# Three of eight experts' output matmuls in two float32r parts, with the two halves of PSUM added on GpSimd

## The chip, the cores and the metric

The kernel runs on one NeuronCore of one Trainium2 chip. The metric is the device time of one execution in microseconds (us), smaller is better. Five engines work beside one another, each through its own queue in order: TensorE (PE in the profile, with its weight loads as PEld), VectorE (DVE), ScalarE (ACT), GpSimd (POOL) and SyncE (SP), which here only issues DMA transfers.

## The reference, cut to what matters

```python
# x: (4, 4160, 192), weight_gen: (4, 4160, 8, 7)
w = softmax(weight_gen, axis=-1)                       # 7 taps, 8 heads
x_pad = concatenate([zeros(B, 6, D), x], axis=1)
out = einsum('bshk,bskhg->bshg', w, x_unf)             # 7 shifted rows of x, 24 channels a head
x = out.reshape(B, S, 192)

h = maximum(x @ w_in, 0.0)                             # 192 -> 1024
conv_out = sum_k conv_w[k] * hp[:, k:k + S, :]         # 3 taps along the sequence
gate = 1.0 / (1.0 + exp(-conv_out))
return (h * gate) @ w_out                              # 1024 -> 192
```

Everything is float32. What the change's name calls experts are the eight slices (NF = 8) of 128 columns into which the kernel cuts the 1024 hidden columns; `f` counts them.

## The kernel before

The 16640 positions lie on 128 partitions with 130 positions each (SEG). One step `j` handles four positions of every partition (R = 4), 512 columns once they are transposed; there are 33 steps (NB).

**Attention, step q.** `load_x` brings rows of x into `ring`, a ring of 24 rows (RING), and `load_w` brings the tap weights of two steps into one of four buffers (WB = 4), where `sm_ops` makes the softmax. `tap` (L292) multiplies rows of the ring by a tap's weights: seven products a step, in steps q >= 3 all on GpSimd. Two accumulating DMAs (`fold1`, `fold2`, issued by GpSimd) and one GpSimd addition (`fold3`, L325) sum the seven products, PE transposes the sum (L340, 6 matmuls a step), and `split_hi` (ACT, L360) and `split_lo` (DVE, L364) leave it as a pair of float32r tiles, H the rounded values and L what the rounding left.

**Unit (j, f).** `mm1` (L378) makes 128 hidden columns for 512 positions with five float32r matmuls of 512 columns into one of five PSUM buffers `z` (NZ = 5). Then `relu` (ACT, L384) writes h, `wmid` (ACT, L388) the middle tap of the convolution back into z, `conv_side` twice (DVE, L395) the side taps, `sig` (ACT, L402) a tanh, and `gmul` (DVE, L411) the gated value into `g` in SBUF, which frees z. `carry` (SP, L416) copies the last two rows of h to where the next step needs them.

**Output tile (j, i).** For each of a step's four positions `mm2` (L424) adds up eight float32 matmuls, one for each slice f, with 128 columns of g as the stationary operand and 192 columns of `wo` as the moving one. A float32 matmul is two MATMUL records in the trace, so a tile has 16. `evac` (ACT, L433) copies the tile from PSUM to `o` with a factor 0.5, and `store` (SP, L437) writes the four tiles of a step. Two PSUM buffers (`ops`, `dps`) take turns.

**Order.** All of this is first collected as tasks with a duration and dependences (`task`, durations from `vec`, `act`, `pool` and constants such as `d_ = 0.03 + NF * 0.326` for an output tile), a list scheduler places the tasks, and the instructions are issued in that order, which is fixed from then on. Tiles of step j are ranked at j + 1.62 (`WO_`), attention of step q at q - 2.7 (`TO`). A task of kind "VK" holds both DVE and GpSimd in the plan.

Of the kernel before, what the change touches and what calls it, by code (L numbers as in the profile page):

```python
# [35 lines left out]
WB = 4  # L36
ROUNDS = 1
RING = 24
CG = 2
CH = (  # L40
# [11 lines left out]
def vec(n, ps=1):  # L52

    return 0.07 + n / 960 + 0.06 * ps
# [11 lines left out]
def kernel(  # L66
# [37 lines left out]
    o_p = ctx.enter_context(tc.tile_pool(name="o", bufs=4))  # L104
# [10 lines left out]
    wh, wl = wi[:, 0], wi[:, 1]  # L115
    wo = const.tile([P, NF, D], F32, name="wo")
    h = const.tile([P, NF, R + 2, P], F32, name="h")
# [248 lines left out]
    z_t, g_t = {}, {}  # L366
# [36 lines left out]

    def g_of(j, f):
        if j not in g_t:
            g_t[j] = g_p.tile([P, NF, W], F32, tag="g", name="g")
        return g_t[j][:, f, :geom(j)[0] * P]
# [12 lines left out]
    def mm2(j, i, ps=None):  # L420
        if ps is None:
            ps = (ps_d if i % 2 else ps_o).tile([P, W], F32, tag="dps" if i % 2 else "ops", name="ops")
        for f in range(NF):
            nc.tensor.matmul(  # L424
                out=ps[:, 0:D], lhsT=g_of(j, f)[:, i * P:(i + 1) * P], rhs=wo[:, f, :],
                start=(f == 0), stop=(f == NF - 1),
            )
        return j, i, ps

    def evac(j, i, ps):  # L430
        if i == 0:
            o_t[j] = o_p.tile([P, R, D], F32, tag="o", name="o")
        nc.scalar.activation(out=o_t[j][:, i, :], in_=ps[:, 0:D], func=ACTF.Copy, scale=0.5)  # L433

    def store(j, a, b):
        c0 = R * j - 2 if j else 0
        nc.sync.dma_start(  # L437
            out=os_[:, (c0 + a) * D:(c0 + b) * D], in_=o_t[j][:, a:b].rearrange("p s d -> p (s d)")
        )
# [3 lines left out]
    with tc.manual_schedule():  # L443
        stage = g_p.tile([P, NF, W], I32, tag="g", name="stage").rearrange("p f w -> p (f w)")
        r_in = stage[:, 0:2 * FF].rearrange("p (c b) -> p c b", b=2)
        r_fold = stage[:, 2 * FF:3 * FF].rearrange("p (c b) -> p c b", b=2)
        r_cw = stage[0:3 * NF, 3 * FF:3 * FF + 2 * P].rearrange("p (c b) -> p c b", b=2)
        r_out = [o_p.tile([P, 2 * D, 2], I32, tag="o", name="r_out") for _ in range(4)]
# [206 lines left out]


# [69 lines left out]
        zl, last_mm, mm_end = [], [None], {}  # L726

        def unit(j, f):
# [13 lines left out]
            rd[n] = gm[n] = task("V", vec(m_, 0), [t_] + dep, lambda: gmul(j, f))  # L742
            zl.append(gm[n])
# [9 lines left out]
        def out_tiles(j):  # L753
            d_ = 0.03 + NF * 0.326
            no = geom(j)[0]
            for i in range(no):
# [4 lines left out]
                def fn(i=i, hold=hold, z_=z_):  # L761
# [3 lines left out]
                    "P", d_, [rd[j * NF + f] for f in range(NF)] + wo_rdy + dep, fn,  # L765
# [162 lines left out]
```

## Time and profile before

| what | value |
|---|---|
| median of 3 runs | 706.98 us (706.78 to 707.1) |
| span of the profiled execution | 704.3 us, 10972 instructions |
| what lies around the span, by the median | 2.7 us (706.98 - 704.3) |
| PE busy | 683.6 us, 97% |
| DVE busy | 629.0 us, 89% |
| ACT busy | 554.5 us, 79% |
| POOL busy | 514.9 us, 73% |

The profiled execution has no time of its own beside its span; the median of the runs less the span is taken for what lies around it. The span is what the trace covers, from the first to the last instruction. Busy times are unions of the recorded durations; the records of neighbouring instructions on an engine can overlap, so the distance from one start to the next is often shorter than the recorded duration.

### The profile page before, as it was taken

What the parts mean: (1) busy time and instruction counts of PE and PEld (TensorE: products, weight loads), DVE (VectorE), ACT (ScalarE), POOL (GpSimd) and SP (SyncE); (2) the same over time, 40 slices, a digit from 0 to 9 for tenths busy, and PEclk for the clock granted to TensorE, in tenths of its full rate; (3) what the DMA queues carried; (4) which work ended last, traced back from release to release, by engine and by line L of the source; (5) the groups of instructions that cost most, each with busy time, mean ns of one, the idle gap of its engine ahead of it and who ended that gap; (6) DMA issues with size and microseconds to landing.
All of it is one profiled execution on the core that took longest, in us unless ns stands there. A gap on an engine that the chain in (4) does not pass through costs nothing.

```text
span 704.3 us, 10972 instructions
## 1 busy us (share of the span) xinstructions
PE 683.6 (97%) x3749; PEld 623.3 (89%) x3749; DVE 629.0 (89%) x1005; ACT 554.5 (79%) x1079; POOL 514.9 (73%) x422
## 2 busy tenths in 40 slices
PE   1899999999999999999999999999999999999998
PEld 1788999999999999999999999999999999999998
DVE  6999999999999999999899899988898888888881
ACT  3588888887888888878787787888878778888881
POOL 3998987998999888897776878877777788730000
PEclk9999999999999999999999999999999999999999
DMA  7736998999999888797988889788888887781211
GB/s 236 214 92 166 218 205 207 211 226 213 207 223 217 202 199 194 178 207 170 218 190 201 197 163 223 176 213 193 189 188 184 177 184 167 171 194 67 78 44 45
DMA packets 70787, 127.59 MB, mean 181 GB/s; under 512 B 5046, under 2 KB 42573, under 8 KB 70732
## 3 DMA queue, kind: packets, MB, share of 16 engines
q0 software_dynamic: 20160, 58.99, 47.5%
q1 hardware_dynamic: 50090, 67.51, 29.6%
q8 instruction: 29, 0.48, 0.3%
q10 hardware_dynamic: 482, 0.40, 0.2%
q14 instruction: 26, 0.21, 0.1%
HBM read 20.51 MB, written 12.78 MB: 47 GB/s over the span
## 4 chain that ended last, share of the span: by engine, by line
PE 96%; DVE 2%; DMA 1%; POOL 0%; issue 0%; ACT 0%; POOLq 0%
PE ops L424 47%; PE z L378 43%; PE tp L340 4%; PE ops L340 1%; DMA stage<-in_moe_conv_w_dram 1%; PE z L424 1%; DMA stage<-in_moe_w_in_dram 0%; DVE py L292 0%; POOL px L292 0%; POOL py L292 0%; DVE r L257 0%; DVE m L248 0%; DVE w L242 0%; DVE px L292 0%; DVE dps L146 0%
## 5 line engine op out<-in xcount | busy, mean ns | idle before, releaser
L395 DVE SCALAR_TENSOR_TENSOR z<-h,cw,z 128x512 f32<-128x512 f32 (+1 forms) x528 | 377.6, 742 | 21.6 <-ACT z L388 15.7
L424 PE MATMUL ops<-wo,g 128*128 128x192 f32 x2048 | 353.1, 326 | 0.0
L424 PEld LDWEIGHTS ops<-wo,g 128*128 128x128 f32 x2048 | 338.9, 190 | 9.8
L378 PE MATMUL z<-H,wi 128*128 128x512 f32 x1056 | 303.8, 409 | 1.0 <-ACT wi L614 1.0
L292 POOL TENSOR_TENSOR px<-ring,w 128x768 f32<-128x768 f32 (+2 forms) x146 | 230.9, 1698 | 67.2 <-PE tp L340 67.0
L378 PEld LDWEIGHTS z<-H,wi 128*128 128x128 f32 x1056 | 191.1, 188 | 32.8 <-ACT wi L614 1.4
L402 ACT ACTIVATE z<-z 128x512 f32<-128x512 f32 (+1 forms) x264 | 150.7, 571 | 53.4 <-DVE z L395 51.7
L411 DVE SCALAR_TENSOR_TENSOR g<-z,h 128x512 f32<-128x512 f32 (+1 forms) x264 | 177.0, 678 | 12.3 <-ACT z L402 10.3
L388 ACT ACTIVATE z<-h,cw 128x512 f32<-128x512 f32 (+1 forms) x264 | 179.7, 684 | 6.2
L384 ACT ACTIVATE h<-z 128x512 f32<-128x512 f32 x264 | 155.4, 591 | 15.8 <-PE z L378 15.6
L292 POOL TENSOR_TENSOR py<-ring,w 128x768 f32<-128x768 f32 (+2 forms) x108 | 163.3, 1826 | 2.2 <-DMA px<-py 2.2
L378 PE MATMUL z<-L,wi 128*128 128x512 f32 x264 | 103.0, 390 | 0.0
L325 POOL TENSOR_TENSOR px<-px 128x512 f32<-128x512 f32 (+1 forms) x60 | 72.9, 1466 | 5.3 <-DMA px<-px 5.3
L360 ACT ACTIVATE H<-tp 64x256 fp32r<-64x256 f32 (+1 forms) x93 | 42.3, 454 | 22.0 <-PE tp L340 21.7
L378 PEld LDWEIGHTS z<-L,wi 128*128 128x128 f32 x264 | 49.5, 188 | 11.2
L433 ACT ACTIVATE o<-ops 128x192 f32<-128x192 f32 x128 | 42.1, 329 | 19.2 <-PE ops L424 16.7
L318 POOL DMA_DIRECT2D px<-px x30 | 36.7, 1224 | 15.3 <-DMA px<-py 12.9
L315 POOL DMA_DIRECT2D px<-py x30 | 40.4, 1346 | 8.5 <-POOL py L292 8.5
L340 PE MATMUL tp<-ident,px 128*128 128x128 f32 x228 | 38.0, 281 | 2.8 <-POOL px L292 2.0
L340 PEld LDWEIGHTS tp<-ident,px 128*128 128x128 f32 x228 | 30.0, 145 | 8.7 <-POOL px L292 2.5
L364 DVE TENSOR_TENSOR H<-tp,H 64x256 fp32r<-64x256 f32 x60 | 25.4, 423 | 7.7 <-ACT H L360 5.8
L364 DVE TENSOR_TENSOR L<-tp,H 128x512 fp32r<-128x512 f32 x33 | 22.7, 688 | 8.7 <-ACT H L360 8.6
(67 smaller groups left out, 181.4 us busy)
## 6 DMA issues: line engine op xcount, KB each, us to landing
px<-py POOLq DMA_DIRECT2D x30, 1152.0 KB, 9.9
h<-h SPq DMA_DIRECT2D x128, 256.0 KB, 4.4
px<-px POOLq DMA_DIRECT2D x30, 768.0 KB, 6.6
ring<-in_x_dram SPq DMA_DIRECT2D x31, 384.0 KB, 6.7
out_dram<-o SPq DMA_DIRECT2D x31, 384.0 KB, 5.8
w<-in_weight_gen_dram SPq DMA_DIRECT2D x15, 224.0 KB, 6.0
r_out<-in_moe_w_out_dram SPq DMA_DIRECT2D x4, 384.0 KB, 5.6
wi<-scr SPq DMA_DIRECT2D x8, 128.0 KB, 6.2
```

The lines of the kernel that those rows point to most:

```text
L292: eng.tensor_tensor(out=dst[:, a:b, :].rearrange("p s (h g) -> p s h g", g=GRP), in0=ring[:, p:p + n, :].rearrange("p s (h g) -> p s h g", ...
L325: nc.gpsimd.tensor_tensor(out=dst.rearrange("p (s d) -> p s d", s=R), in0=a[:, :, lo:hi], in1=b[:, :, lo:hi], op=ALU.add)
L340: nc.tensor.matmul(o, lhsT=a, rhs=ident, is_transpose=True, start=(start and c == 0), stop=(stop and c == len(ops) - 1))
L360: nc.scalar.activation(out=hi, in_=src, func=ACTF.Copy)
L364: nc.vector.tensor_tensor(out=lo, in0=src, in1=hi.bitcast(F32), op=ALU.subtract)
L378: nc.tensor.matmul(out=z, lhsT=w[:, fs], rhs=h_t[j, nm], start=(i == 0), stop=(i == len(terms) - 1))
L384: nc.scalar.activation(out=hrow(f, 2, R), in_=z_t[j, f], func=ACTF.Relu)
L388: nc.scalar.activation(out=z_t[j, f][:, :no * P], in_=hrow(f, cc, no), func=ACTF.Copy, scale=cw[:, NF + f:NF + f + 1])
L395: nc.vector.scalar_tensor_tensor(out=z, in0=hrow(f, cc + d, no), scalar=cw[:, k * NF + f:k * NF + f + 1], in1=z, op0=ALU.mult, op1=ALU.add,)
L402: nc.scalar.activation(out=z, in_=z, func=ACTF.Tanh, scale=0.5)
L411: nc.vector.scalar_tensor_tensor(out=g_of(j, f), in0=z_t[j, f][:, :no * P], scalar=1.0, in1=hrow(f, cc, no), op0=ALU.add, op1=ALU.mult)
L424: nc.tensor.matmul(out=ps[:, 0:D], lhsT=g_of(j, f)[:, i * P:(i + 1) * P], rhs=wo[:, f, :], start=(f == 0), stop=(f == NF - 1),)
```

## The change

In steps 2 to 31 (`FIRST = 2`, `LAST = 1`) the matmuls of `mm2` for f = 0, 1, 2 (`NS = 3`) are no longer float32. `w_split` cuts the weights of these slices once into `wos`: a rounded float32r part (ACT) and the rest (DVE). `g_hi` (ACT) rounds the gated value to float32r, `g_lo` subtracts to get the rest, on DVE for f = 0 and 1 and on GpSimd for f = 2 (`GL = "VVG"`). Each slice then takes two float32r matmuls: the rounded part of g against both parts of the weights side by side (384 columns), and the rest of g against the rounded weights (192 columns, added to the first half). The tile's result so stands in two halves of 192 columns; `evac` copies both, and `join` adds them on GpSimd before `store`. For f = 0 and 1 `gmul` writes back into z in PSUM, which stays taken until `g_lo`; for f = 2 it writes into a scratch tile. To find room in SBUF the ring has 20 rows in place of 24, the tap weights three buffers in place of four, and `o` two buffers of double size in place of four.

```diff
--- before.py
+++ after.py
@@ -33,10 +33,14 @@
 NX = 3
 NY = 2
 NZ = 5
-WB = 4
+WB = 3
 ROUNDS = 1
-RING = 24
+RING = 20
 CG = 2
+NS = 3
+GL = "VVG"
+FIRST = 2
+LAST = 1
 CH = (
     ("f", 0, 256, 5.2, "VGP", "G"),
     ("m", 0, 256, 8.7, "VVP", "G"),
@@ -101,7 +105,8 @@
     py_p = ctx.enter_context(tc.tile_pool(name="py", bufs=NY))
     t_p = ctx.enter_context(tc.tile_pool(name="t", bufs=2))
     g_p = ctx.enter_context(tc.tile_pool(name="g", bufs=2))
-    o_p = ctx.enter_context(tc.tile_pool(name="o", bufs=4))
+    gx_p = ctx.enter_context(tc.tile_pool(name="gx", bufs=2))
+    o_p = ctx.enter_context(tc.tile_pool(name="o", bufs=2))
     ps_z = ctx.enter_context(tc.tile_pool(name="ps_z", bufs=NZ, space=bass.MemoryType.PSUM))
     ps_t = ctx.enter_context(tc.tile_pool(name="ps_t", bufs=1, space=bass.MemoryType.PSUM))
     ps_o = ctx.enter_context(tc.tile_pool(name="ps_o", bufs=1, space=bass.MemoryType.PSUM))
@@ -113,7 +118,9 @@
     cw = const.tile([P, 3 * NF], F32, name="cw")
     wi = const.tile([P, 2, 2, FF], F32R, name="wi")
     wh, wl = wi[:, 0], wi[:, 1]
+    NP = NF - NS
     wo = const.tile([P, NF, D], F32, name="wo")
+    wos = const.tile([P, NS, 2, D], F32R, name="wos")
     h = const.tile([P, NF, R + 2, P], F32, name="h")
     cw_raw = h[0:3 * NF, 0, R, :]
     ring = const.tile([P, RING, D], F32, name="ring")
@@ -363,7 +370,7 @@
         for src, hi, lo in parts(q, part, tp, pairs):
             nc.vector.tensor_tensor(out=lo, in0=src, in1=hi.bitcast(F32), op=ALU.subtract)
 
-    z_t, g_t = {}, {}
+    z_t, g_t, gs_t, gx_t = {}, {}, {}, {}
 
     def geom(j):
         no = R if j else R - 2
@@ -401,10 +408,42 @@
         z = z_t[j, f][:, :geom(j)[0] * P]
         nc.scalar.activation(out=z, in_=z, func=ACTF.Tanh, scale=0.5)
 
+    def halves(j):
+        return FIRST <= j < NB - LAST
+
+    def split(j, f):
+        return f < NS and halves(j)
+
+    def gx_of(j, f, b):
+        if j not in gx_t:
+            gx_t[j] = gx_p.tile([P, NS, 2, W], F32R if halves(j) else F32, tag="gx", name="gx")
+        return gx_t[j][:, f, b, :geom(j)[0] * P]
+
     def g_of(j, f):
+        if split(j, f):
+            if GL[f] == "G":
+                n = gs_t.setdefault((j, f), len(gs_t))
+                return scr[n % 2][:, n // 2 % 3].bitcast(F32)
+            return z_t[j, f]
+        if f < NS:
+            return gx_of(j, f, 0)
         if j not in g_t:
-            g_t[j] = g_p.tile([P, NF, W], F32, tag="g", name="g")
-        return g_t[j][:, f, :geom(j)[0] * P]
+            g_t[j] = g_p.tile([P, NP, W], F32, tag="g", name="g")
+        return g_t[j][:, f - NS, :geom(j)[0] * P]
+
+    def g_hi(j, f):
+        nc.scalar.activation(out=gx_of(j, f, 0), in_=g_of(j, f), func=ACTF.Copy)
+
+    def g_lo(j, f):
+        (nc.vector if GL[f] == "V" else nc.gpsimd).tensor_tensor(
+            out=gx_of(j, f, 1), in0=g_of(j, f), in1=gx_of(j, f, 0).bitcast(F32), op=ALU.subtract
+        )
+
+    def wo_hi():
+        nc.scalar.activation(out=wos[:, :, 0], in_=wo[:, 0:NS], func=ACTF.Copy)
+
+    def wo_lo():
+        nc.vector.tensor_tensor(out=wos[:, :, 1], in0=wo[:, 0:NS], in1=wos[:, :, 0].bitcast(F32), op=ALU.subtract)
 
     def gmul(j, f):
         no, cc = geom(j)
@@ -420,32 +459,44 @@
     def mm2(j, i, ps=None):
         if ps is None:
             ps = (ps_d if i % 2 else ps_o).tile([P, W], F32, tag="dps" if i % 2 else "ops", name="ops")
+        c = slice(i * P, (i + 1) * P)
+        terms = []
         for f in range(NF):
-            nc.tensor.matmul(
-                out=ps[:, 0:D], lhsT=g_of(j, f)[:, i * P:(i + 1) * P], rhs=wo[:, f, :],
-                start=(f == 0), stop=(f == NF - 1),
-            )
+            if split(j, f):
+                terms.append((2 * D, gx_of(j, f, 0)[:, c], wos[:, f].rearrange("p b d -> p (b d)")))
+                terms.append((D, gx_of(j, f, 1)[:, c], wos[:, f, 0]))
+            else:
+                terms.append((D, g_of(j, f)[:, c], wo[:, f, :]))
+        for n, (m, g, w) in enumerate(terms):
+            nc.tensor.matmul(out=ps[:, 0:m], lhsT=g, rhs=w, start=(n == 0), stop=(n == len(terms) - 1))
         return j, i, ps
 
     def evac(j, i, ps):
         if i == 0:
-            o_t[j] = o_p.tile([P, R, D], F32, tag="o", name="o")
-        nc.scalar.activation(out=o_t[j][:, i, :], in_=ps[:, 0:D], func=ACTF.Copy, scale=0.5)
+            o_t[j] = o_p.tile([P, 2, R, D], F32, tag="o", name="o")
+        n = 2 if halves(j) else 1
+        nc.scalar.activation(
+            out=o_t[j][:, 0:n, i, :], in_=ps[:, 0:n * D].rearrange("p (b d) -> p b d", b=n), func=ACTF.Copy, scale=0.5
+        )
+
+    def join(eng, j, a, b):
+        o = o_t[j]
+        eng.tensor_tensor(out=o[:, 0, a:b], in0=o[:, 0, a:b], in1=o[:, 1, a:b], op=ALU.add)
 
     def store(j, a, b):
         c0 = R * j - 2 if j else 0
         nc.sync.dma_start(
-            out=os_[:, (c0 + a) * D:(c0 + b) * D], in_=o_t[j][:, a:b].rearrange("p s d -> p (s d)")
+            out=os_[:, (c0 + a) * D:(c0 + b) * D], in_=o_t[j][:, 0, a:b].rearrange("p s d -> p (s d)")
         )
 
     V, G = nc.vector, nc.gpsimd
 
     with tc.manual_schedule():
-        stage = g_p.tile([P, NF, W], I32, tag="g", name="stage").rearrange("p f w -> p (f w)")
+        stage = gx_p.tile([P, NS, 2, W], I32, tag="gx", name="stage").rearrange("p f b w -> p (f b w)")
         r_in = stage[:, 0:2 * FF].rearrange("p (c b) -> p c b", b=2)
         r_fold = stage[:, 2 * FF:3 * FF].rearrange("p (c b) -> p c b", b=2)
-        r_cw = stage[0:3 * NF, 3 * FF:3 * FF + 2 * P].rearrange("p (c b) -> p c b", b=2)
-        r_out = [o_p.tile([P, 2 * D, 2], I32, tag="o", name="r_out") for _ in range(4)]
+        r_cw = g_p.tile([P, NP, W], I32, tag="g", name="r_cw")[0:3 * NF, 0, 0:2 * P].rearrange("p (c b) -> p c b", b=2)
+        r_out = [t[:, i] for t in [o_p.tile([P, 2, 2 * D, 2], I32, tag="o", name="r_out") for _ in range(2)] for i in range(2)]
         w_in_i = w_in.bitcast(I32).rearrange("k (f b) -> k f b", b=2)
 
         def load_in(eng, kind, a, b):
@@ -653,6 +704,10 @@
             last_use[iB] = last_use[iC] = [j_]
             wo_rdy.append(j_)
 
+        def w_split():
+            a_ = task("A", act(NS * D), wo_rdy, wo_hi)
+            return [task("VK", vec(NS * D, 0), [a_], wo_lo)]
+
 
         spl_done, all_taps, tiles, gm, rd, ca, mm = {}, {}, {}, {}, {}, {}, {}
         xf_, yf_, gp = [], [], [None]
@@ -723,7 +778,7 @@
             if yend:
                 yf_.append(task("none", 0.0, yend))
 
-        zl, last_mm, mm_end = [], [None], {}
+        zl, last_mm, mm_end, gl_ = [], [None], {}, []
 
         def unit(j, f):
             n = j * NF + f
@@ -739,8 +794,16 @@
             cv_ = task("V", vec(m_), [cv_], lambda: conv_side(j, f, 0, -1))
             t_ = task("A", act(m_) + 0.02, [cv_], lambda: sig(j, f))
             dep = [tiles[j - 2, i] for i in range(geom(j - 2)[0])] if j >= 2 else wo_rdy if j else []
-            rd[n] = gm[n] = task("V", vec(m_, 0), [t_] + dep, lambda: gmul(j, f))
-            zl.append(gm[n])
+            sp = split(j, f)
+            temp = sp and GL[f] == "G"
+            rd[n] = gm[n] = task(
+                "V", vec(m_, 0), [t_] + (gl_[-6:][:1] if temp and len(gl_) > 5 else [] if sp else dep), lambda: gmul(j, f))
+            if sp:
+                a_ = task("A", act(m_), [gm[n]] + dep, lambda: g_hi(j, f))
+                rd[n] = task("G", pool(m_), [a_], lambda: g_lo(j, f)) if temp else task("V", vec(m_, 1), [a_], lambda: g_lo(j, f))
+                if temp:
+                    gl_.append(rd[n])
+            zl.append(rd[n] if sp and not temp else gm[n])
             f0 = f // CG * CG
             ns = [j * NF + f0 + i for i in range(CG)]
             if j + 1 < NB and all(k in gm for k in ns):
@@ -751,7 +814,8 @@
         zfree, last_evac, stored = [], [], []
 
         def out_tiles(j):
-            d_ = 0.03 + NF * 0.326
+            hv = halves(j)
+            d_ = 0.03 + NF * 0.326 - 0.042 * NS * hv
             no = geom(j)[0]
             for i in range(no):
                 now[0] = j + WO_ + i / R
@@ -762,9 +826,9 @@
                     hold[0] = mm2(j, i, ps_z.tile([P, W], F32, tag="z", name="z") if z_ else None)
                 dep = [mm[NU - 1], (zl + zfree)[-NZ]] if z_ else bank[1 + i % 2]
                 a_ = tiles[j, i] = task(
-                    "P", d_, [rd[j * NF + f] for f in range(NF)] + wo_rdy + dep, fn,
+                    "P", d_, [rd[j * NF + f] for f in range(NF)] + (ws_rdy if hv else wo_rdy) + dep, fn,
                     after=[tiles.get((j, i - 1))])
-                e_ = task("A", act(D) + 0.02, [a_] + (stored[-4:][:1] if i == 0 and len(stored) > 3 else []),
+                e_ = task("A", act(D * (1 + hv)) + 0.02, [a_] + (stored[-2:][:1] if i == 0 and len(stored) > 1 else []),
                           lambda hold=hold: evac(*hold[0]), begun=last_evac)
                 last_evac[:] = [e_]
                 if z_:
@@ -773,6 +837,8 @@
                     bank[1 + i % 2] = [e_]
                 if j == NB - 1 and i % 2 == 1:
                     dma(0.5, [e_], lambda i=i: store(j, i - 1, i + 1))
+            if hv:
+                e_ = task("G", pool(no * D), [e_], lambda: join(G, j, 0, no))
             if j < NB - 1:
                 stored.append(dma(1.2, [e_], lambda: store(j, 0, no)))
 
@@ -781,6 +847,8 @@
             loads(q)
             head(q)
 
+        now[0] = FIRST - 1.5
+        ws_rdy = w_split()
         attention(0)
         attention(1)
         for j in range(NB):
```

## Rows read from the trace of the kernel before

**Rows 1.** The page: busy time by engine; TensorE's granted clock in 40 slices.

```profile
PE 683.6 (97%) x3749; PEld 623.3 (89%) x3749; DVE 629.0 (89%) x1005; ACT 554.5 (79%) x1079; POOL 514.9 (73%) x422
...
PEclk9999999999999999999999999999999999999999
```

**Rows 2.** Busy time of the engines by stretch of the span, in us.

```profile
core 0: us, PE busy (x) PEld busy (x) DVE busy (x) ACT busy (x) POOL busy (x), PEclk, DMA share, GB/s
0.00:60.00 60.00, 42.38 (x257) 36.05 (x258) 52.09 (x117) 37.62 (x82) 46.28 (x46) 1.00 0.59 167
60.00:200.00 140.00, 140.00 (x763) 128.06 (x762) 132.94 (x206) 115.91 (x226) 126.48 (x105) 1.00 0.94 215
200.00:340.00 140.00, 140.00 (x762) 127.98 (x761) 130.56 (x203) 115.88 (x227) 118.95 (x96) 1.00 0.88 198
...
620.00:704.00 84.00, 81.18 (x452) 75.32 (x450) 61.04 (x93) 57.29 (x110) 3.18 (x3) 1.00 0.28 82
```

**Rows 3.** The chain that ended last, 300 to 345 us: start, us, what.

```profile
301.76 2.60 PE ops L424 x16
304.36 3.43 PE z L378 x15
...
316.43 0.44 PE tp L340 x4
...
320.62 0.22 PE tp L340 x2
...
322.00 2.60 PE ops L424 x16
```

**Rows 4.** Groups by line and shape, whole span: busy us, mean ns, idle before.

```profile
L364 DVE TENSOR_TENSOR L<-tp,H 128x512 fp32r<-128x512 f32 x33 | 22.7, 688 | 8.7 <-ACT H L360 8.6
...
L340 PE MATMUL ops<-ident,px 128*64 128x128 f32 x48 | 8.4, 310 | 0.0
```

**Rows 5.** PE and DMA on the chain of the start, 0 to 75 us.

```profile
22.25 1.51 POOL px L292
...
50.18 0.44 PE ops L340 x4
```

**Rows 6.** DVE in order of time, 349 to 356 us: start, us, instruction.

```profile
351.50 0.68 DVE L411 SCALAR_TENSOR_TENSOR g<-z,h 128x512 f32<-128x512 f32 x1
352.11 0.74 DVE L395 SCALAR_TENSOR_TENSOR z<-h,cw,z 128x512 f32<-128x512 f32 x1
352.76 0.68 DVE L411 SCALAR_TENSOR_TENSOR g<-z,h 128x512 f32<-128x512 f32 x1
```

**Rows 7.** ACT in order of time, 300 to 325 us.

```profile
300.42 0.33 ACT L433 ACTIVATE o<-ops 128x192 f32<-128x192 f32 x1 [0.34 <-PE ops L424]
300.64 0.76 ACT L360 ACTIVATE H<-tp 64x256 fp32r<-64x256 f32 x2
...
316.90 0.60 ACT L360 ACTIVATE H<-tp 128x512 fp32r<-128x512 f32 x1 [1.04 <-PE tp L340]
317.40 0.59 ACT L384 ACTIVATE h<-z 128x512 f32<-128x512 f32 x1
```

**Rows 8.** POOL in order of time, 300 to 322 us.

```profile
303.95 1.19 POOL L318 DMA_DIRECT2D px<-px  x1
304.73 1.99 POOL L292 TENSOR_TENSOR px<-ring,w 128x768 f32<-128x768 f32 x1
306.24 4.97 POOL L292 TENSOR_TENSOR py<-ring,w 128x768 f32<-128x768 f32 x3
311.50 1.28 POOL L315 DMA_DIRECT2D px<-py  x1 [0.30 <-POOL py L292]
312.32 2.45 POOL L325 TENSOR_TENSOR px<-px 128x512 f32<-128x512 f32 x2
314.25 2.02 POOL L292 TENSOR_TENSOR px<-ring,w 128x768 f32<-128x768 f32 x1
315.75 1.44 POOL L242 TENSOR_TENSOR w<-w,m 128x448 f32<-128x448 f32 x1
320.92 1.55 POOL L292 TENSOR_TENSOR px<-ring,w 128x768 f32<-128x768 f32 x1 [3.73 <-PE tp L340]
```

**Rows 9.** The page's DMA issues: count, KB each, us to landing.

```profile
h<-h SPq DMA_DIRECT2D x128, 256.0 KB, 4.4
...
ring<-in_x_dram SPq DMA_DIRECT2D x31, 384.0 KB, 6.7
```

## The prediction

> **What bounds the kernel now.** I read the page's busy times first: PE is busy for 97% of the span at the full clock, 2.4 GHz, in every slice [rows 1]. A share of the whole span does not yet say that PE sets the time, so the second view is the table by stretch: from 60 us on PE is busy for 140.00 of every 140.00 us, and what PE idles lies in the first 60 us (17.6 us) and at the very end (2.8 us) [rows 2]. No other engine is that full: DVE by its records up to 95%, POOL up to 90%, ACT 83% [rows 2]. The third view is the chain that ended last, and in its middle it is nothing but PE. There one step can be read off: from one output tile at 301.76 us to the same tile of the next step at 322.00 us are 20.24 us. A tile's 16 records take 2.60 us, three units' 15 matmuls take 3.43 us, and the six transposes of a step take 0.44 + 0.22 us [rows 3]. Four tiles (10.40), eight units (8 x 1.14 to 1.16, together 9.2) and 0.66 give 20.26 us, so nothing is left over for waits. The time of this kernel is PE's column time, 33 steps of it behind a start. Anything taken from PE between step 2 and step 31 shortens the time one for one, as long as the others keep up.
>
> **What the change takes from PE.** A float32 matmul of 192 columns is 2.60 / 8 = 0.325 us [rows 3]. In 30 steps x 4 tiles x 3 slices, 360 of them give way to a pair of float32r matmuls of 384 and of 192 columns. No row shows float32r at these widths. The nearest are the five 512-column float32r matmuls of a unit: 3.43 / 15 = 0.229 us each [rows 3], that is 0.447 ns a column. By columns 384 cost 0.172 us and 192 cost 0.086 us. The longer one I take at 0.172: it lies close to the row. The shorter one is bounded from below by these columns, 0.086, and from above by the float32 price of the same width, 0.325. Between these far ends it depends on whether the 128 x 128 weight load behind each matmul still hides under so short a stream. The closest rows are transposes, a load each and 128 columns: 4 in 0.44 us, so a load and its matmul fit into 0.109 us [rows 3]. Transposes that load 64 columns take the same 0.44 us for four [rows 4, 5], so 0.109 is a ceiling for the load and not shown to be the load itself. I take 0.110 for the 192-column matmul, the shortest distance at which any row shows PE changing its weights. The pair is 0.172 + 0.110 = 0.282 us, the saving 0.043 us, and 360 x 0.043 = 15.5 us. A tile falls from 2.60 to 2.47 us, a step from 20.24 to 19.72 us.
>
> A page bears on the open term. In the Trainium skill, "TensorE: Matmul & The Clock Gate", section on LDWEIGHTS, a load takes one cycle of 1.2 GHz for each column, which is an estimate of 107 ns for 128 columns; by it the pair would be 0.279 us and the saving 16.6 us. The same page's section on Fast Weight Load says that 128 weights of a type other than FP32 are loaded in four parallel parts, by which the load would hide and the pair would cost its columns alone. The rows here tell neither apart, since they agree with a load of anything up to 109 ns.
>
> **What it adds elsewhere, per step, against 19.72 us.** DVE: 16 side taps at 0.65 us from start to start, 8 gate products at 0.61 [rows 6], the splits and half a softmax make 17.7 us now. Two subtractions of the shape of L364 (recorded 0.69 us [rows 4]; as they stand between the 0.61 and 0.65 of their neighbours, 0.63) add 1.26, and two gate products that write to PSUM rather than SBUF add 0.04 each, the difference of these two rows. That is 19.0 us, 96%. ACT: three more copies to float32r at 0.50 us [rows 7] add 1.5; the four evacuations grow from 192 to 384 columns, each by between nothing and the 0.28 us that separate 0.22 (evacuation to next start) from 0.50 [rows 7], and I take 0.16, so 0.6 in all. ACT goes from 16.8 us (83% of 20.24) to 18.9 us, 96% by records that overlap. POOL: now 7 products at 1.50, fold1 0.82, fold2 0.78, fold3 1.93 [rows 8], the broken products at the ring's end and half a softmax, 15.1 us; it has 3.7 us to spare a step, in which it waits for PE to free px [rows 8]. The subtraction of f = 2 has the size of fold3's first part, which is at most 1.24 (1.93 x 512 / 768 gives 1.29 as a check), and join, 768 elements, lies between a product's 1.50 and fold3's 1.93; I take 1.25 + 1.7. That is 18.1 us, 92%. All three fit, but PE would now have three neighbours above 90% where it had none, and their order is fixed. I book 1.0 us of PE waiting over the 30 steps for it; nothing below and the 4 us of rival 2 above are its ends.
>
> **Edits that cost nothing, and their cover.** The longer hold of z: two of eight units keep their buffer some 1.4 us longer (a copy and a subtraction). Five buffers for eight units a step are 12.3 us for each; the chain from mm1 to the gate product is some 6 us by these rows, so there are about 5 us of cover. The store of a step now waits for join on POOL instead of for an evacuation on ACT, and behind the waiting store in SP's queue stand the carries, 4.4 us to landing [rows 9], for which the next step's relu waits; a carry has most of a step, and a join that POOL starts 5 us late still leaves half of that. If POOL were a whole step behind, the relu would be late, then z, then PE. The ring of 20 rows lets a load of x start only when the products of two steps earlier are done; it lands in 6.7 us [rows 9], while the products of the step between keep POOL for 10.5 us (7 x 1.50). At the start the same rule loads x for step 2 a second time, after the last product of step 0 at 23.8 us [rows 5], and it is there before step 1's products end at about 34 us. One more product in 42 is broken in two at the ring's end, 0.02 us a step on POOL. Three buffers of tap weights for groups of two steps leave a load three to four steps. Two double-size buffers of `o` give the store a whole step, against some 6 us of transfer. What is not hidden is `w_split`: 576 columns once on ACT (about 0.5 us) and on DVE, while GpSimd is held, about 0.7 us, in a start where PE waits for both. Between nothing and 1.2 us; I book 1.0.
>
> **The sum.** Against the profiled execution: 704.3 - 15.5 + 1.0 + 1.0 = 690.8 us of span, and with the 2.7 us around it 693.5 us against the median of 706.98.
>
> **The rivals.** First, the short stream hides its load: the 192-column matmul costs its columns, 0.086 us, the pair 0.258, the saving is 0.067 x 360 = 24.1 us and the time 685. For it speaks that 512 columns take hardly more than a column's share; against it, that no row has PE changing weights faster than every 0.109 us.
>
> Second, an elementwise engine becomes the bound. If DVE's recorded durations were what it needs, its 130.56 us in 140 us [rows 2] are 18.9 us a step, and two subtractions of 0.69 and the dearer products make that 20.3, above the present 20.24: no gain, and over 30 steps up to 4 us lost on the step, time up to 711. Against it: the starts lie 0.61 and 0.65 us apart where the records say 0.68 and 0.74 [rows 6], so the records overlap. The same can come from ACT, by late relus, or from POOL, by a join that stops the carries. In between, PE would wait 0.2 to 0.5 us a step and the time would be 700 to 709; I take 704 for this case. The trace would show PE waiting for DVE's or ACT's work on z in every step.
>
> Third, on the other side: a float32r stream as short as 192 columns runs at the float32 price, 0.325 us. The pair costs 0.497, each slice loses 0.172, and 360 x 0.172 = 61.9 us more give 769. It decides from 0.153 us upward (0.325 - 0.172) for that one matmul. For it speaks only that all float32r rows of this trace are 512 columns wide, so nothing excludes a price by width; against it, that nothing in the rows hints at one.
>
> **How the numbers follow.** PE still bound and the pair near 0.282: 0.60, with 689 to 698 as its own range; the load hidden: 0.08; an elementwise engine or SP's queue eats most of the gain: 0.17; the short stream at float32 price: 0.13; anything else, no change or a little slower: 0.02. The predicted time is the first case's, 693.5 us. From 684 to 706 lie the first case, most of the hidden-load case and about 0.1 of the elementwise-engine case's 0.17, some 0.78 in all; the dear short stream and the slow side of the elementwise case are left out. A change under 0.2% (1.4 us) can't be told from none here. Faster: 0.60 + 0.08 + 0.10 of the 0.17 = 0.78. Within 0.2%: 0.03 (time within 1.4 us of 707, from the elementwise-engine case). Slower: 0.13 + 0.04 + 0.02 = 0.19.
>
> **What would show it.** The step, from tile to tile, at 19.7 us; the tile at 2.47 us, with 384-column records some 0.17 us and 192-column ones 0.11 us from start to start; PE without waits from 60 us on; DVE and ACT at 95% or more of each stretch, POOL still waiting for px. The forecast is wrong if the 192-column record stands at 0.09 or above 0.15 us, or if PE waits for z or for `tp` appear in every step. The plan books 0.042 us a slice for PE; if the chip's price is far from that, the fixed order fits worse, and waits will show even where sums fit.

## The result and the profile after

The changed kernel takes 714.88 us (711.76 to 716.41, four runs) against 707.04 us of the kernel before on the same chip: a ratio of 1.0101, with a 95% interval of 1.0076 to 1.0127. It is slower by 1%, clear of the noise; 693.5 us had been forecast, with chances of 0.78 for faster and 0.19 for slower. Run once more beside the last experiments it took 715.90 us (1.0124, 1.0107 to 1.0140). The profiled execution took 714.61 us, of which the span is 712.9 us.

First the busy time of the engines by stretch, as in [rows 2]:

```profile
core 0: us, PE busy (x) PEld busy (x) DVE busy (x) ACT busy (x) POOL busy (x), PEclk, DMA share, GB/s
60.00:200.00 140.00, 135.90 (x743) 122.28 (x744) 132.76 (x213) 122.67 (x239) 135.63 (x109) 1.00 0.90 202
200.00:340.00 140.00, 135.85 (x743) 122.90 (x743) 132.86 (x212) 124.15 (x242) 138.00 (x109) 0.99 0.85 195
340.00:480.00 140.00, 138.66 (x766) 124.70 (x765) 132.80 (x210) 124.73 (x240) 126.55 (x101) 1.00 0.83 192
480.00:620.00 140.00, 137.22 (x748) 123.29 (x747) 130.77 (x206) 123.91 (x239) 133.25 (x105) 0.99 0.83 187
```

PE is no longer busy for all of a stretch; 12.4 us are missing in these four. POOL, at 126.48 and 118.95 us before, now stands at 135.63 and 138.00 us in the first two: level with PE in the first, and above every other engine in the second.

The chain that ended last still is nothing but PE in its middle, as in [rows 3]:

```profile
306.41 2.48 PE ops L471 x16
308.88 1.16 PE z L385 x5
310.05 0.22 PE tp L347 x2
310.26 2.48 PE ops L471 x16
...
326.23 2.48 PE ops L471 x16
```

So where nothing disturbs PE the change does what it was meant to do: a tile takes 2.48 us in place of 2.60, and from one tile (306.41) to the same tile of the next step (326.23) are 19.82 us in place of 20.24. Read off by steps (from the end of one step's last unit on PE to that of the next), before had 20.24 in nearly each; after has 19.57 and 20.05 in turn, or 19.79, but also 24.2 (step 2), 21.3 (4), 25.5 (10), 21.5 (20) and 25.2 us (24). The 31 steps from step 2 to the end add up to 634.7 us against 626.6. Undisturbed they would be 30 x 19.8 + 19.1 = 613.1 us. So 13.5 us were saved and 21.6 lost, and the three longest steps alone hold 15.5 of these. Over the 31 steps (columns as above):

```profile
59.32:693.95 634.63, 621.59 (x3405) 560.44 (x3406) 600.24 (x948) 563.51 (x1081) 559.60 (x442) 0.99 0.80 185
```

PE idles for 13.0 of the 21.6 us; before, it was busy for all 626.57 us of the same steps. Some 3 us more are the two stretches at a lower clock that follow the pauses of steps 10 and 24 (an estimate: 4 us at a mean of 0.63 from 244 us on, as shown below, and 4 us at 0.57 from 523 us on). The other 5 us or so lie in steps that are longer with hardly a gap between PE's records; what they are is not shown.

What PE and its neighbours waited for, from 60 to 640 us (engine, line, releaser: us in total, times, longest):

```profile
POOL px L325 <- DMA px<-py: 22.1, 10, 4.0
ACT h L391 <- DMA h<-h: 16.8, 8, 5.6
...
PE z L385 <- DVE gx L438: 6.5, 4, 3.8
...
PE z L385 <- DVE g L450: 2.5, 1, 2.5
```

Before, POOL's greatest wait was for PE (67.0 us, for `tp`) and that for fold1's transfer (px<-py) 12.9 us; the wait for PE is gone, so POOL has used up its lead. ACT's relu waits for carries (h<-h), which it never did in this window before. One long step shows how these hang together. The chain of step 10:

```profile
224.18 1.33 DVE z L402 x2
...
225.52 11.18 DMA h<-h
...
236.78 0.60 ACT h L391
237.38 1.19 ACT z L395 x2
...
241.66 0.60 DVE gx L438
242.26 0.04 issue
242.30 1.45 PE z L385 x5
```

A carry issued at 225.52 us lands 11.18 us later, the relu starts with it, then wmid, the side taps, the gate and the subtraction follow one another, and PE gets its z buffer at 242.30, after 3.84 us with nothing to do. What SP and POOL did meanwhile (start, us, instruction; a DMA's row is its issue):

```profile
213.53 5.07 SPq L455 DMA_DIRECT2D h<-h  x2
223.81 0.33 SPq L206 DMA_DIRECT2D w<-in_weight_gen_dram  x1
224.19 1.23 SPq L176 DMA_DIRECT2D ring<-in_x_dram  x1
225.52 0.98 SPq L455 DMA_DIRECT2D h<-h  x1
226.92 0.34 SPq L488 DMA_DIRECT2D out_dram<-o  x1
```

```profile
220.88 2.90 POOL L299 TENSOR_TENSOR px<-ring,w 128x768 f32<-128x768 f32 x1
222.37 2.65 POOL L322 DMA_DIRECT2D px<-py  x1
223.19 3.70 POOL L484 TENSOR_TENSOR o<-o 128x768 f32<-128x768 f32 x1
225.00 2.82 POOL L249 TENSOR_TENSOR w<-w,m 128x448 f32<-128x448 f32 x1
225.93 3.14 POOL L438 TENSOR_TENSOR gx<-scr,gx 128x512 fp32r<-128x512 f32 x1
...
236.61 1.22 POOL L325 DMA_DIRECT2D px<-px  x1 [0.20 <-issue]
```

SP stands from 218.6 to 223.81 us before the load of tap weights, which may start only when POOL's product of 220.88 is done (it ends at 223.78). Behind that load stand a load of x, the carry and a store, and all are let go within some 3 us, into the transfer of fold1 that POOL issued at 222.37. How long transfers issued from 215 to 240 us took (count, KB each, us from issue to landing):

```profile
px<-py POOLq DMA_DIRECT2D x1, 1152.0 KB, 13.9
...
ring<-in_x_dram SPq DMA_DIRECT2D x1, 384.0 KB, 10.0
out_dram<-o SPq DMA_DIRECT2D x1, 384.0 KB, 10.7
```

By the page's medians these are 10.8, 4.6 and 7.3 us over the whole run, and a carry's is 4.9. So all of them landed late together, the carry among them; that they got in each other's way is the likely reading, and no run takes it apart. Step 24 shows the same road: SP waits 8.2 us for POOL at a load of weights, until 506.84, and the carry behind it lands late, while the relu waits 5.6 us for it:

```profile
509.31 12.17 DMA h<-h
```

From 60 to 640 us SP's waits for POOL, at the load of weights and at the store behind the join, came to

```profile
SPq L206 <- POOL px L299: 52.7, 10, 8.7
...
SPq L488 <- POOL o L484: 41.1, 17, 6.0
```

The first was 24.9 us in 10 times before; the second is new. PE's pause has a second price (stretches around it, columns as above):

```profile
228.00:236.00 8.00, 8.00 (x42) 7.02 (x41) 6.68 (x11) 4.18 (x8) 8.00 (x7) 1.00 1.08 251
236.00:242.00 6.00, 2.47 (x16) 2.17 (x15) 3.77 (x6) 5.18 (x11) 5.80 (x7) 1.00 1.01 249
...
244.00:248.00 4.00, 4.00 (x20) 4.00 (x18) 4.00 (x8) 3.18 (x7) 3.22 (x4) 0.63 0.56 164
```

PE idled, and then the granted clock fell for some microseconds, from 1.00 to a mean of 0.63, so it was at the 1.2 GHz level for most of that stretch. The tile that began at 244.61 us took 3.67 us in place of 2.48.

### The profile page after: what moved, and what is told of

It reads as the page before. It is cut to its first block, busy times and chain, and to the rows that moved or that the text cites. A ratio compares the mean times of both kernels' runs of the same rounds, so it can differ in the third digit from the quotient of the medians.

```text
span 712.9 us, 11282 instructions
## 1 busy us (share of the span) xinstructions
PE 679.0 (95%) x3749; PEld 610.4 (86%) x3749; DVE 655.0 (92%) x1067; ACT 604.6 (85%) x1170; POOL 606.5 (85%) x488
## 4 chain that ended last, share of the span: by engine, by line
PE 45%; DVE 17%; POOL 15%; DMA 13%; ACT 5%; issue 5%; ACTq 0%; DVEq 0%; POOLq 0%
PE ops L471 23%; PE z L385 20%; DMA h<-h 8%; DVE z L402 8%; POOL px L299 5%; POOL py L299 5%; DMA px<-py 3%; ACT h L391 2%; DVE g L450 2%; PE tp L347 2%; DVE z L450 2%; DVE gx L438 1%; ACT z L395 1%; ACT z L409 1%; POOL px L332 1%
## 5 line engine op out<-in xcount | busy, mean ns | idle before, releaser
L299 POOL TENSOR_TENSOR px<-ring,w 128x768 f32<-128x768 f32 (+3 forms) x149 | 246.1, 1948 | 0.5
L471 PE MATMUL ops<-wo,g 128*128 128x192 f32 x1280 | 232.2, 329 | 0.0
L471 PEld LDWEIGHTS ops<-wo,g 128*128 128x128 f32 x1280 | 205.7, 190 | 0.0
L299 POOL TENSOR_TENSOR py<-ring,w 128x768 f32<-128x768 f32 (+3 forms) x110 | 181.7, 1962 | 1.3 <-DMA px<-py 1.3
L391 ACT ACTIVATE h<-z 128x512 f32<-128x512 f32 x264 | 156.3, 595 | 25.7 <-DMA h<-h 16.8
L471 PE MATMUL ops<-wos,gx 128*128 128x384 f32 x720 | 122.0, 305 | 0.0
L484 POOL TENSOR_TENSOR o<-o 128x768 f32<-128x768 f32 x30 | 80.7, 2690 | 48.4 <-issue 26.9
L471 PEld LDWEIGHTS ops<-wos,gx 128*128 128x128 f32 x720 | 113.6, 191 | 8.8
L450 DVE SCALAR_TENSOR_TENSOR g<-z,h 128x512 f32<-128x512 f32 (+1 forms) x165 | 111.1, 679 | 10.7 <-ACT z L409 8.2
L478 ACT ACTIVATE o<-ops 128x384 f32<-128x384 f32 (+1 forms) x128 | 60.5, 478 | 11.7 <-PE ops L471 9.5
L325 POOL DMA_DIRECT2D px<-px x30 | 44.2, 1475 | 22.8 <-DMA px<-py 22.1
L438 POOL TENSOR_TENSOR gx<-scr,gx 128x512 fp32r<-128x512 f32 x30 | 56.0, 1866 | 5.2 <-ACT gx L435 4.0
## 6 DMA issues: line engine op xcount, KB each, us to landing
px<-py POOLq DMA_DIRECT2D x30, 1152.0 KB, 10.8
```

The source lines that it names most:

```text
L299: eng.tensor_tensor(out=dst[:, a:b, :].rearrange("p s (h g) -> p s h g", g=GRP), in0=ring[:, p:p + n, :].rearrange("p s (h g) -> p s h g", ...
L391: nc.scalar.activation(out=hrow(f, 2, R), in_=z_t[j, f], func=ACTF.Relu)
L438: (nc.vector if GL[f] == "V" else nc.gpsimd).tensor_tensor(out=gx_of(j, f, 1), in0=g_of(j, f), in1=gx_of(j, f, 0).bitcast(F32), op=ALU.sub ...
L450: nc.vector.scalar_tensor_tensor(out=g_of(j, f), in0=z_t[j, f][:, :no * P], scalar=1.0, in1=hrow(f, cc, no), op0=ALU.add, op1=ALU.mult)
L471: nc.tensor.matmul(out=ps[:, 0:m], lhsT=g, rhs=w, start=(n == 0), stop=(n == len(terms) - 1))
L478: nc.scalar.activation(out=o_t[j][:, 0:n, i, :], in_=ps[:, 0:n * D].rearrange("p (b d) -> p b d", b=n), func=ACTF.Copy, scale=0.5)
```

## The experiments

The theories, by the letters of the expectations: A, GpSimd has too much work; B, the smaller buffers (ring of 20 rows, three weight groups) hold up loads; C, DVE or ACT is the bound, as their work grew; D, SP's queue, in which a load that waits for GpSimd stands before the carries. A theory of the order, E, came later: the fixed order books transfers too short. In brackets behind each time stand its ratio to the kernel before and the 95% interval.

**no_join.**
```diff
-                e_ = task("G", pool(no * D), [e_], lambda: join(G, j, 0, no))
+                pass
```


> The changed kernel without join: the two halves of a tile are not added, and store writes the first half alone, so the second half's share of the output is left out. PE, ACT and DVE keep all their work. Theory A, GpSimd sets the pace (recorded busy for 135 to 138 of 140 us, 18.2 us of spacings a step plus the waits for fold1's transfer): 1.8 us a step go from GpSimd, PE's long idle stretches go, 693 to 698 us. Theory B, the smaller buffers (ring of 20, three weight groups) hold SP's queue and with it the carries: little change, 707 to 713. Theory C, DVE or ACT is the bound: no change, 713 to 716.

Measured: 707.58 us (1.0011, 0.9988 to 1.0034). Seven us come back, but not what A forecast. The profiled execution is one of the slower of its ten (711.48 us; the fastest took 705.15). In it carries still land late (its chain, at two places):

```profile
304.33 11.43 DMA h<-h
...
505.98 11.78 DMA h<-h
```

and the work taken from POOL turned into waiting for fold1: `px L325 <- DMA px<-py` rose from 22.1 to 58.7 us. An engine that waits 59 us for a transfer is not held up by its work alone, so A as it stood is too simple.

**bufs_only** (the kernel before with the two sizes alone).
```diff
-WB = 4
+WB = 3
-RING = 24
+RING = 20
```


> The kernel before with nothing changed but RING = 20 and WB = 3. Theory A (GpSimd's load): 706 to 708 us, since GpSimd has 3.7 us a step to spare there. Theory B (the buffers): 711 us or more, with PE waiting in the middle of the span.

Measured: 709.83 us (1.0039, 1.0025 to 1.0054). From step 8 on all steps are 20.24 us; what it costs is some 2.8 us, most of it in the start, the rest at one step near 180 us and at the end. In that kernel, then, B is a part and not the cause.

**lo_on_dve.**
```diff
-GL = "VVG"
+GL = "VVV"
```


> The changed kernel with the third subtraction on DVE rather than GpSimd (GL = VVV): GpSimd loses 1.24 us a step, DVE gains 0.60. Theory A: GpSimd falls to some 17 us of spacings a step, 695 to 702 us. Theory B: 709 to 714, since join and the buffers stay. Theory C, DVE is the bound (18.4 us of spacings a step by the trace of after, 19.0 with this): slower than 715.

Measured: 707.33 us (1.0001, 0.9985 to 1.0016). DVE has more to do (138.49 of 140 us from 200 to 340 us) and the kernel is faster by about 8 us, which speaks against C and for relief of GpSimd, though by less than A said. POOL's wait for fold1 rose here too, from 22.1 to 39.3 us. Late carries (7.8 us of relu waits) and steps up to 24.2 us remain; steps 2 to 6 alone take 108.8 us in place of 99, which is most of what is still lost.

**three_192** (three matmuls of 192 columns for each slice, all adding to the same half, so that no join is needed; not shown here: `evac` copies 192 columns and `join` is left out).
```diff
-                terms.append((2 * D, gx_of(j, f, 0)[:, c], wos[:, f].rearrange("p b d -> p (b d)")))
+                terms.append((D, gx_of(j, f, 0)[:, c], wos[:, f, 0]))
+                terms.append((D, gx_of(j, f, 0)[:, c], wos[:, f, 1]))
```


> The changed kernel with three float32r matmuls of 192 columns for each slice in place of one of 384 and one of 192, all into the same columns of PSUM, so that join falls away and evac copies 192 columns. It measures the price of a short float32r matmul. If each costs some 0.11 us, as the pair's 0.283 us says when 384 columns are 0.172, a slice costs 0.33, no less than float32: a tile of 2.60 to 2.64 us, a step of 20.2 to 20.4, 708 to 713 us. If it costs the 0.087 us that stand between the records of after, a tile is 2.41 us and the time 690 to 697.

Measured: 716.16 us (1.0125, 1.0103 to 1.0147). The chain of waits:

```profile
304.26 2.63 PE ops L472 x19
306.89 1.16 PE z L385 x5
```

Nine short matmuls and five float32 ones make a tile of 2.63 us. With 0.325 for each float32 one, (2.63 - 1.625) / 9 = 0.112 us for 192 columns. That is more than their 0.086 by columns, far from the float32 price, and close to the 0.109 of a transpose of 128 columns [rows 3]: the price hardly follows the width here, and that it is the change of weights that one pays for fits this and is not shown apart. PE is busy for all of 140 us from 200 us on, at 20.37 us a step. So without a gain on PE nothing waits, but POOL has no join to do here either; it waits 22.3 us for fold1, as long as in after, and the relu only 0.5 us for carries. The time lies above its forecast of 708 to 713 us, as step 2 takes 24.2 us here too.

**two_slices, two_slices_again, two_slices_bufs, two_slices_third.** Two split slices, without GpSimd's subtraction; then again; with the old buffer sizes; and split from step 3 on. (Not shown here: the start's staging tiles change pools.)
```diff
-NS = 3
-GL = "VVG"
+NS = 2
+GL = "VV"
```


> The changed kernel with two slices in two parts instead of three, both subtractions on DVE (NS = 2, GL = VV), with the small buffers. PE's saving is two thirds, 30 x 4 x 2 x 0.043 = 10.3 us; GpSimd keeps join and loses its subtraction, DVE is as in the changed kernel. Theory A: 697 to 700 us. Theory B: 705 to 710, the stalls of the buffers stay. Theory C: 700 to 706.

> The kernel of two_slices once more, beside the others on one chip, for its ratio: 0.989 to 0.993 of the kernel before, 700 to 701 us.

> Two slices in two parts, with the ring of 24 rows and four weight groups of the kernel before, for which there is room then. If the buffers cost what bufs_only showed (2.5 us, nearly all in the start), 697.5 to 698.5 us, with the third step at 20 to 21 us instead of 22.8. If the start's loss comes from the split of the weights or the new work of step 2, 700 to 701 as with the small buffers.

> Two slices in two parts from step 3 on rather than from step 2 (FIRST = 3). One step's saving of 0.33 us is given up. If the long third step (22.8 us) comes from the work that the split puts into step 2, it falls to some 20.5 us and the time to 698.5 to 699.5; if it comes from the start itself, 701.

Measured: 700.63 us (0.9910, 0.9890 to 0.9930), 700.56 (0.9895, 0.9880 to 0.9909), 703.23 (0.9943, 0.9926 to 0.9959) and 702.35 us (0.9923, 0.9904 to 0.9943). Two slices save less on PE and gain, just short of what A forecast; the stretches of two_slices:

```profile
200.00:340.00 140.00, 140.00 (x775) 127.87 (x774) 136.43 (x215) 127.17 (x242) 130.83 (x103) 1.00 0.88 201
340.00:480.00 140.00, 140.00 (x774) 127.81 (x773) 136.77 (x217) 126.37 (x239) 124.55 (x100) 1.00 0.86 197
```

Each step from the fifth on takes 19.91 us, close to 20.24 less 8 x (0.325 - 0.285) = 0.32. PE doesn't stop there with DVE at 136 of 140 us, which speaks against C again, although the time also lies in C's range. Old buffer sizes don't improve it, which is one more word against B; the last two kernels took longer than either of their forecasts. Step 2 takes 22.7 to 22.9 us in all of them, with old buffers and with step 2 not split as well.

**w_on_pool** (GpSimd issues the weight loads from group 3 on, so that SP needn't wait for it).
```diff
-                softmax(g, dma(0.7, all_taps[g0] + (all_taps[g0 - 1] if g0 else []), lambda: load_w(g)))
+                softmax(g, dadd(all_taps[g0] + (all_taps[g0 - 1] if g0 else []), 0.7, lambda: load_w(g, nc.gpsimd), 0.8))
```


> The changed kernel with one thing moved: the loads of the tap weights (from group 3 on) are issued by GpSimd, which makes the products that they wait for, and no longer by SP, where they stood in front of the carries. GpSimd pays some 0.8 us for every second step. Theory D, SP's queue (a load that waits for GpSimd's products holds the carries behind it, 52.7 us in the trace of after): the late carries go, 700 to 706 us. Theory A, GpSimd is simply overfull: 714 us or more.

Measured: 728.71 us (1.0294, 1.0257 to 1.0331). Relu waits for carries fell from 16.8 to 3.5 us, as D wanted, but `ACT o L478 <- DMA out_dram<-o` is 19.6 us and PE waits 9.3 us for `tp` behind DVE's split and 3.6 us behind POOL; steps go up to 27.2 us. The time is in A's range, but the whole order is another one here, so this refutes only that moving the issue is a remedy.

**fold_late_plan, fold_late_q6s, fold_late_q8.** The same instructions, and another order: the planner books a fold's transfer longer, in all steps (6.2 in place of 3.2), from step 6 on (4.7) and from step 8 on (6.2). The edit of the last:
```diff
-            return task("none", 3.2, [task("D", occ, [task("G", e, deps, fn)])])
+            return task("none", 3.2 if now[0] - TO < 8 else 6.2, [task("D", occ, [task("G", e, deps, fn)])])
```


> The changed kernel with one number of the plan altered: the time from a fold's DMA to its landing is booked 3 us longer (6.2 for 3.2). No instruction is added or taken away, only the fixed order differs. Theory E, the order counts on transfers that come earlier than they do (fold1 lands after 10.8 us in the median, single ones after 14): GpSimd waits less for fold1, 700 to 708 us. Theory A, the work itself is too much: 712 to 717.

> As fold_late_q8, but 1.5 us later in place of 3, and from attention step 6. fold1's landing is then booked at 11.2 us, which is its median here, with nothing for the late ones. Theory E: between the changed kernel and fold_late_q8, 701 to 709 us. Theory A: 710 or more.

> The changed kernel with the folds' landing booked 3 us later in the plan from attention step 8 on; before that the plan is as it was, and no instruction is added or taken away. Theory E, the order counts on transfers earlier than they come: the first eight steps lose the 5 us that they lose in the changed kernel, and the long steps after them (25.5, 21.5, 25.2 us) go: 700 to 703 us, with every step from the twelfth on at 19.6 to 20.1. Theory A, the work is too much for GpSimd: the stalls come back in other places, 710 or more.

Measured: 707.51 us (1.0001, 0.9990 to 1.0011), 704.73 (0.9961, 0.9950 to 0.9972) and 703.92 us (0.9944, 0.9927 to 0.9960). The stretches of fold_late_q8:

```profile
200.00:340.00 140.00, 137.25 (x758) 123.59 (x757) 134.88 (x215) 126.75 (x246) 138.14 (x110) 1.00 0.85 197
340.00:480.00 140.00, 140.00 (x779) 127.08 (x778) 135.70 (x216) 128.10 (x247) 135.39 (x109) 1.00 0.86 201
480.00:620.00 140.00, 140.00 (x780) 127.18 (x779) 135.77 (x213) 128.66 (x246) 132.79 (x105) 1.00 0.85 194
```

and its waits from 60 to 640 us:

```profile
ACT h L391 <- DMA h<-h: 5.7, 6, 2.9
...
POOL px L325 <- DMA px<-py: 4.1, 3, 1.8
```

From 340 us on PE never stops, with steps of 19.57 and 20.05 us, while POOL does all its work and is as busy as in after. So the three slices fit. In the two others PE is busy for 139.7 us or more of each 140 us from 200 to 620, so this is no luck of one order. POOL's wait for fold1 fell from 22.1 to 4.1 us, the relu's for carries from 16.8 to 5.7, and the time by some 11 us: with the same work, it was the order. The forecast of fold_late_q8 was just missed, since steps 12 and 13 still take 21.6 and 21.2 us. Booked late from the first step on, the start suffers (steps 2 and 3 take 27.2 and 25.6 us), and of the gain over after some 7 us stay.

**carry_single, q8_single.** One carry for each slice in place of one for two, in after and in fold_late_q8.
```diff
-CG = 2
+CG = 1
```


> The changed kernel with a carry for each slice rather than one for two (CG = 1): the carry of the first slice of a pair starts a unit earlier, some 2.5 us, and is half as large; SP issues twice as many. If late carries are what hands the other queues' lateness to PE, the long stalls shrink: 703 to 710 us. If PE would wait for z or the transposes anyway, 713 to 716; if the larger number of transfers costs more than it gives, above that.  PE, DVE, ACT and GpSimd have the same work.

> fold_late_q8 with a carry for each slice: there the carries are hardly waited for after step 12, so 701 to 704 us, no clear difference from fold_late_q8 (703.9); more if 128 further transfers disturb.

> The changed kernel once more, on the chip of these runs, for comparison: 712 to 717 us, with three or more steps above 21 us after the third, at much the same places, since the order is fixed.

Measured: 713.42 us (1.0084, 1.0069 to 1.0099), 700.93 (0.9906, 0.9891 to 0.9921), and after_again, the changed kernel as it is, 715.90 us (above). In carry_single the relu waits 8.3 us for carries, step 10 falls from 25.5 to 21.2 us and step 24 from 25.2 to 22.4, as wanted, and step 26 stalls instead (24.9). The chain of that stall doesn't lead to a carry:

```profile
555.39 5.21 DVE r L268
...
561.92 3.89 PE z L385 x10
```

One small DVE instruction takes 5.3 us and holds up z; the last section comes back to it. Without that stall this execution would have taken some 709 us (an estimate: 713.98 less the 5.1 by which 24.9 exceeds 19.8), in the range that was forecast for late carries. So carry_single speaks more for the carries than its time says. In q8_single PE is busy for all of every stretch from 200 to 620 us, with three slices. The relu there waits for no carry that the profile counts from 60 to 640 us.

The two best, two_slices (700.6) and q8_single (700.9), beat the kernel before by some 1% and the changed one by 2%. The buffer sizes of before with three split slices were not tried; there is no room for both.

## Why the prediction was wrong

**The price on PE was right.** The pair costs (2.48 - 5 x 0.325) / 3 = 0.285 us against the 0.282 of the forecast, a tile 2.48 against 2.47, a step 19.8 against 19.72. That took 13.5 us off the 31 steps, where 15.5 had been booked. The value for the 192-column matmul, 0.110, was chosen by the nearest row, four transposes in 0.44 us, and three_192 gives 0.112. With it the first rival falls (load hidden, 0.086) and the third (float32 price, 0.325), which held most of the chance for slower. The runs now also lean to one of the two rules that the prediction named: 0.112 us lies close to the estimate of 107 ns that the Trainium skill's "TensorE: Matmul & The Clock Gate" gives in its section on LDWEIGHTS, and the hidden load that its section on Fast Weight Load would give to a type other than FP32 isn't seen for float32r.

**The added work was sized right.** In after, from start to start: the join 1.80 us (223.19 to 225.00; booked 1.7), the subtraction on POOL 1.23 (225.93 to 227.16; 1.25), on DVE 0.60 (0.63), and the start with `w_split` is 0.3 us longer (booked 1.0). POOL was put at 18.1 us a step, 92% of 19.72; in the first 140 us of rows above it is 97% by its records, in the third stretch 90%.

**The step that failed** is "Edits that cost nothing, and their cover", and with it the 1.0 us that "All three fit" booked for PE's waiting, where the steps lost 21.6 us, 13.0 of them as idle time of PE: 704.3 - 13.5 + 21.6 + 0.3 and 0.2 at the end give the 712.9 us of span. Three statements there are wrong. "A carry has most of a step" was taken from the issue to landing of 4.4 us [rows 9] against a step of 20; by the trace of before the time from a carry's issue to the relu that needs it is 8.6 us at least and 11.6 in the median, after 7.1 and 11.1. So a carry that lands in 11 to 12 us, as in steps 10 and 24, stops the relu, and a carry that is issued behind a load that waits for POOL does so the sooner. "Three buffers of tap weights" were said to leave a load three to four steps; but SP stood for 52.7 us in all at these loads, until POOL's products were done, with the carries behind them in its queue. The prediction had looked there only for a store that waits for join, which cost SP another 41.1 us. And POOL's sum counted only its instructions. It also has to wait for fold1's transfer before it issues fold2: fold1 lands 10.8 us after issue in the median, and 13.9 in step 10. In the order as written, POOL has other work meanwhile, but a fixed amount; where the transfer takes longer, POOL waits, and with 92% of its time spoken for it has little room to catch up as it could before, when it was ahead of PE by 67.0 us of waits for `tp`.

**The second rival** named the road (an engine besides PE, or SP's queue, by a join that stops the carries, then late relus) and priced it at 700 to 709 us, by waits of 0.2 to 0.5 us in every step. What came were a few stalls of 4 to 6 us, with late transfers and a lower clock on top, and not a share in each step; that DVE's recorded durations become the bound, its first half, lo_on_dve speaks against.

**What shows the cause.** The order, with a POOL that has little room: fold_late_q8 has the instructions of after, and its PE runs without a stop from 340 us on; no_join and lo_on_dve, with less for POOL to do (and an order planned anew for that), gave back 7 and 8 us. That late carries carry the delay to PE is shown in the chains of steps 10 and 24. That POOL's waits for fold1 are the root isn't shown: they fell from 22.1 to 4.1 us along with the time in fold_late_q8, but rose to 58.7 in no_join and 39.3 in lo_on_dve, which are faster than after, and were 22.3 in three_192, where PE never stops from 200 us on. Each rebooking moves everything else too, and w_on_pool shows how much that alone can cost. **Open** is the start: step 2 takes 22.7 to 27.2 us in every kernel with the split and 20.0 in before, and 20.2 with the small buffers alone; neither the old sizes, nor leaving step 2 unsplit, nor single carries bring it back. In after PE idles there twice, for 1.84 us before an output tile, behind DVE's split, and for 1.81 us before z; two_slices_third has only waits for z and two_slices_bufs one for `tp`, so it isn't one wait alone. This step is most of what q8_single's span (698.3) lacks against the forecast of 690.8: 25.7 - 19.8 = 5.9 of 7.5 us.

## What to carry to other kernels

A saving on the bound engine is worth what it says only as long as the neighbours keep their lead; where a wait of a neighbour for the bound engine (here POOL's 67.0 us for `tp`) vanishes, ask what its lead had covered, transfers of uncertain length above all. In a fixed order, ask for each transfer what stands before it in its queue and what that waits for, and measure cover from issue to the consumer's start, not as a part of a step. When a change saves on paper and loses on the chip, rebook the transfers or take a smaller part of the change first: here the smaller part, and the rebooking together with single carries, each gave about half of what had been forecast for the whole change.

## What the runs showed of the hardware

Starts of records don't give the price of short matmuls: in after the record of a 384-column matmul and the next one lie 0.17 to 0.20 us apart and those from a 192-column one to the next 0.087, where three_192 prices the latter at 0.112. The two distances together, some 0.28 us, do match the pair's 0.285, so what the records leave open is how it divides; sums over a tile (2.48, 2.63 us) hold.

In carry_single one small DVE instruction, of 128 x 8 elements, took 5.30 us, where the same one takes 0.22 us in before and 0.23 in after (DVE, then POOL, in order of time):

```profile
555.30 5.30 DVE L268 TENSOR_SCALAR r<-r,mask 128x8 f32<-128x8 f32 x1
```
```profile
555.07 3.39 POOL L332 TENSOR_TENSOR px<-px 128x512 f32<-128x512 f32 x2
557.01 4.70 POOL L299 TENSOR_TENSOR px<-ring,w 128x384 f32<-128x384 f32 x4
```

While it stands, POOL's instructions follow one another without a pause, by their records from 552.02 to 561.71 us. The Trainium skill's "SBUF — State Buffer", section "Who interferes with whom", counts tensor_scalar among the DVE operations that can take the port pair shared with GpSimd, and says that the one which comes second is blocked altogether. A DVE record of that length beside POOL's row fits that; that the wait lasts over several POOL instructions the Trainium skill doesn't say there, and no run tested it.
